# Two fp8 double-row matmuls, side by side or apart in a stream of bf16 matmuls

One core of one Trainium2 chip. The metric is device microseconds of one launch.

## The reference

Two stages, one after the other: cross-covariance attention over channels in 4 batches of 6016 tokens by 256 channels, then a gated feed-forward block on its 24064 output rows.

```python
def _attn_ref(q, k, v, tau):                       # 4 x 6016 x 256
    qn = q / (np.linalg.norm(q, axis=1, keepdims=True) + 1e-06)
    kn = k / (np.linalg.norm(k, axis=1, keepdims=True) + 1e-06)
    s = kn.transpose(0, 2, 1) @ qn / tau           # 256 x 256 a batch
    # ... softmax over the last axis -> a
    return v @ a

def _moe_ref(x, w_gate, w_val, w_out):             # 24064 x 256, 1536 wide
    g = x @ w_gate
    return (g * (1 / (1 + np.exp(-g))) * (x @ w_val)) @ w_out
```

## The kernel before

The attention matrix of a batch is multiplied into the gate and value weights (`Wg`, `Wv`), so the rows of v go straight into the feed-forward block. That block is a loop of steps: two gate matmuls and two value matmuls (512 columns each), then four output matmuls (256 columns) of the chunk before. Between the output matmuls of one step and the gate matmuls of the next stands the background work for the next batch, by a plan; among it is the product of q and k in fp8. In the double-row mode one matmul takes both 128-row slices of a pair at once.

```python
    def gemm1_pair(b, t):                       # one pair of 128-row slices
        # ... kq is allocated at t == 0
        for jh in range(CH):                    # CH = 2
            js = slice(jh * P, (jh + 1) * P)
            if pm == 2:
                nc.tensor.matmul(kq[:, jh, :], q_sb[:, ps:ps + 2, js],
                                 k_sb[:, ps:ps + 2, :], ..., perf_mode=DR)
            else:                               # the 47th slice has no partner
                nc.tensor.matmul(kq[:, jh, :], q_sb[:, ps, js], k_sb[:, ps, :], ...)

    def gv_matmuls(b, ci, f):
        # ... g_ps and v_ps from a pool of two buffers each
        for dst, W in ((g_ps, Wg), (v_ps, Wv)):
            for kk in range(CH):
                nc.tensor.matmul(dst[:, :mv], W[:, kk, fs], vT[:, kk, :mv], ...)
        return g_ps, v_ps, mv

    for t in range(NP):                         # NP = 24 pairs
        step = SQ0 + (5 * t) // 2
        plan[step].append((norm_acc, t))
        plan[step + 1].append((gemm1_pair, t))
    # ...
            g_ps, v_ps, mv = gv_matmuls(b, ci, f)
            # ... silu on ACT, product on DVE
            if prev is not None:
                prev.emit(prev.cm)              # four output matmuls
            if b + 1 < B:
                background(b + 1, ci * FH + f)  # the plan's work of this step
```

## Time and profile before

| | before |
|---|---|
| median of 6 runs (lowest to highest) | 815.43 us (815.32 to 816.31) |
| plain step, gate start to gate start | 1300 ns |
| step with a double-row pair, and the step after it | 1522.4 and 1310.9 ns |
| double-row pairs in batches 1 to 3 | 69, and 3 ordinary pairs |

The groups give the parts of TensorE's work that matter here; the columns are line, engine, operation, output and inputs, shapes and count, then busy us and mean ns of one, then idle us before them.

```profile
L463 PE MATMUL o_new<-w_out_sb,sv 128*128 128x256 bf16 x2256 | 338.3, 273 | 0.0
L429 PE MATMUL g_ps<-vT,Wg 128*128 128x512 bf16 (+1 forms) x1128 | 331.1, 375 | 0.0
L429 PE MATMUL v_ps<-vT,Wv 128*128 128x512 bf16 (+1 forms) x1128 | 330.4, 374 | 0.0
...
L149 PE MATMUL kq_new<-k_sb,q_sb 128*128 128x512 fp8e5 x184 | 40.0, 309 | 0.7 <-DMA q_sb<-in_q_dram 0.7
```

An output matmul is recorded with 273 ns, but the next one starts 109 ns after it: records overlap, since a matmul's end is modelled. What TensorE's stream costs is read from starts, not from these durations. The idle time of 0.0 says that nothing is waited for.

### The profile page before, as it was taken

What the parts mean: (1) busy time and instruction counts of PE and PEld (TensorE: products, weight loads), DVE (VectorE), ACT (ScalarE), POOL (GpSimd) and SP (SyncE); (2) the same over time, 40 slices, a digit from 0 to 9 for tenths busy, and PEclk for the clock granted to TensorE, in tenths of its full rate; (3) what the DMA queues carried; (4) which work ended last, traced back from release to release, by engine and by line L of the source; (5) the groups of instructions that cost most, each with busy time, mean ns of one, the idle gap of its engine ahead of it and who ended that gap; (6) DMA issues with size and microseconds to landing.
All of it is one profiled execution on the core that took longest, in us unless ns stands there. A gap on an engine that the chain in (4) does not pass through costs nothing.

```text
span 813.6 us, 13772 instructions
## 1 busy us (share of the span) xinstructions
PE 800.4 (98%) x5037; PEld 487.1 (60%) x5037; DVE 526.7 (65%) x816; ACT 434.9 (53%) x756; POOL 265.8 (33%) x344
## 2 busy tenths in 40 slices
PE   5999999999999999999999999999999999999998
PEld 3656666665565666666565666666656565665666
DVE  4777777667556777756756687765765555555554
ACT  4566655545555656545555556654554544444543
POOL 5515887313000888722000388751300000000000
PEclk9999999999999999999999999999999999999999
DMA  9993875328311678333812368632652112112101
GB/s 88 143 158 69 112 105 88 78 53 122 80 40 46 96 100 105 74 65 88 127 40 59 53 87 118 92 78 66 141 97 66 46 48 57 53 39 65 50 27 59
DMA packets 93220, 64.59 MB, mean 79 GB/s; under 512 B 52593, under 2 KB 92017, under 8 KB 92401
## 3 DMA queue, kind: packets, MB, share of 16 engines
q0 software_dynamic: 19200, 27.01, 28.6%
q1 hardware_dynamic: 73952, 36.71, 17.7%
q8 instruction: 39, 0.64, 0.3%
q14 instruction: 29, 0.23, 0.1%
HBM read 78.64 MB, written 36.70 MB: 142 GB/s over the span
## 4 chain that ended last, share of the span: by engine, by line
PE 95%; DMA 4%; POOL 1%; issue 0%; DVE 0%; POOLq 0%
PE o_new L463 30%; PE g_ps L429 30%; PE v_ps L429 30%; PE ps L398 2%; PE kq_new L149 2%; DMA v_sb<-in_v_dram 1%; DMA k_sb<-in_k_dram 1%; DMA q_sb<-in_q_dram 1%; POOL k_sb L104 1%; PE ps L331 0%; PE unit_ps L398 0%; PE cs L305 0%; PE kq_new L154 0%; PE ps L388 0%; PE vt_ps L128 0%
## 5 line engine op out<-in xcount | busy, mean ns | idle before, releaser
L439 DVE TENSOR_TENSOR sv<-silu,v_ps 128x512 bf16<-128x512 bf16 (+1 forms) x576 | 388.6, 675 | 263.2 <-ACT silu L435 261.4
L435 ACT ACTIVATE silu<-g_ps 128x512 bf16<-128x512 f32 (+1 forms) x576 | 338.6, 588 | 324.6 <-PE g_ps L429 302.0
L463 PE MATMUL o_new<-w_out_sb,sv 128*128 128x256 bf16 x2256 | 338.3, 273 | 0.0
L429 PE MATMUL g_ps<-vT,Wg 128*128 128x512 bf16 (+1 forms) x1128 | 331.1, 375 | 0.0
L429 PE MATMUL v_ps<-vT,Wv 128*128 128x512 bf16 (+1 forms) x1128 | 330.4, 374 | 0.0
L463 PEld LDWEIGHTS <-sv 128*128 128x128 bf16 x2256 | 220.7, 98 | 140.8
L429 PEld LDWEIGHTS <-Wv 128*128 128x128 bf16 x1152 | 112.7, 98 | 130.8 <-ACT Wv L410 0.2
L281 POOL TENSOR_TENSOR acc_new<-acc_new,sq 128x512 f32<-128x512 f32 x135 | 157.3, 1165 | 43.7 <-DVE sq L271 33.7
L429 PEld LDWEIGHTS <-Wg 128*128 128x128 bf16 x1152 | 106.7, 98 | 27.0 <-ACT Wg L410 0.2
L271 DVE TENSOR_TENSOR sq<-q_sb 128x512 bf16<-128x512 fp8e5 x72 | 63.9, 888 | 0.0
L276 POOL TENSOR_TENSOR acc_new<-sq 128x512 f32<-128x512 bf16 x3 | 3.5, 1152 | 150.7 <-DVE sq L271 150.7
L272 ACT ACTIVATE sq<-k_sb 128x512 bf16<-128x512 fp8e5 x72 | 44.2, 614 | 0.0
L149 PE MATMUL kq_new<-k_sb,q_sb 128*128 128x512 fp8e5 x184 | 40.0, 309 | 0.7 <-DMA q_sb<-in_q_dram 0.7
L472 ACT COPY o_sb<-o_new 128x512 f32<-128x512 f32 x48 | 28.1, 586 | 14.9 <-PE o_new L463 14.5
L474 DVE COPY o_sb<-o_new 128x512 f32<-128x512 f32 (+1 forms) x48 | 31.8, 661 | 3.0 <-PE o_new L463 3.0
L104 POOL DMA_DIRECT2D q_sb<-in_q_dram x48 | 27.0, 562 | 13.3 <-DMA k_sb<-in_k_dram 5.4
L104 POOL DMA_DIRECT2D k_sb<-in_k_dram x48 | 26.0, 549 | 11.3 <-DMA w_out_sb<-in_moe_w_out_dram 5.3
L176 PE MATMUL ss_new<-sq,ones_bf 128*128 128x256 bf16 x83 | 17.6, 351 | 9.0 <-ACT sq L166 8.4
L112 POOL DMA_DIRECT2D vb<-in_v_dram x47 | 24.1, 516 | 5.3 <-DMA vb<-in_v_dram 3.2
L149 PEld LDWEIGHTS <-q_sb 128*128 128x256 fp8e5 x184 | 22.1, 138 | 3.1 <-DMA q_sb<-in_q_dram 2.3
L176 PEld LDWEIGHTS <-ones_bf 128*128 128x128 bf16 x83 | 9.8, 121 | 15.7 <-issue 11.4
L351 POOL TENSOR_SCALAR den<-th 128x512 f32<-128x512 f32 x3 | 1.8, 612 | 51.8 <-ACT th L350 51.8
(93 smaller groups left out, 201.7 us busy)
## 6 DMA issues: line engine op xcount, KB each, us to landing
out_dram<-o_sb SPq DMA_DIRECT2D x92, 256.0 KB, 2.4
vb<-in_v_dram POOLq DMA_DIRECT2D x43, 256.0 KB, 5.4
k_sb<-in_k_dram POOLq DMA_DIRECT2D x44, 128.0 KB, 5.8
q_sb<-in_q_dram POOLq DMA_DIRECT2D x44, 128.0 KB, 5.0
w_out_sb<-in_moe_w_out_dram POOLq DMA_DIRECT2D x1, 768.0 KB, 13.5
vb<-in_v_dram POOLq DMA_DIRECT2D x4, 192.0 KB, 3.5
vT<-vb SPq DMA_TRANSPOSE x47, 3.8
w_gate_sb<-in_moe_w_gate_dram POOLq DMA_DIRECT2D x2, 256.0 KB, 7.3
```

The source lines that it names most:

```text
L104: nc.gpsimd.dma_start(out=dst[:, gs:gs + gm, :], in_=src[b].rearrange("(p s) c -> p s c", s=NS)[:, gs:gs + gm, :])
L149: nc.tensor.matmul(kq[:, jh, :], q_sb[:, ps:ps + 2, js], k_sb[:, ps:ps + 2, :], start=(t == 0 and jh == 0), stop=last, perf_mode=DR, skip_ ...
L176: nc.tensor.matmul(state[b, "ss", which], ones_bf, sq[:, s, :], start=(t == 0 and s == 0), stop=(t == t_last and s == pm - 1))
L271: nc.vector.tensor_mul(sq[:, :pm, 0, :], q_sb[:, ps:ps + pm, :], q_sb[:, ps:ps + pm, :])
L272: nc.scalar.activation(sq[:, :pm, 1, :], k_sb[:, ps:ps + pm, :], ACT.Square)
L281: nc.gpsimd.tensor_tensor(out=acc, in0=acc, in1=sq[:, s, :, :], op=ALU.add)
L429: nc.tensor.matmul(dst[:, :mv], W[:, kk, fs], vT[:, kk, :mv], start=(kk == 0), stop=(kk == CH - 1))
L435: nc.scalar.activation(silu[:, :mv], g_ps[:, :mv], ACT.Silu)
L439: nc.vector.tensor_mul(sv[:, f, :mv], silu[:, :mv], v_ps[:, :mv])
L463: nc.tensor.matmul(self.o_ps[:, j % 2, :], self.sv[:, f, j * P:(j + 1) * P], w_out_sb[:, f, :], start=(f == 0), stop=(f == FH - 1))
L472: nc.scalar.copy(o_sb[:, :m, :], self.o_ps[:, :m, :])
L474: nc.vector.tensor_copy(o_sb[:, :m, :], self.o_ps[:, :m, :])
```

## The change

The matmuls of a pair leave the plan. The first goes behind the two gate matmuls, the second behind the two value matmuls of the same step. The likely intent: a double-row matmul loads twice the weights, and this longer load is to lie under a 512-column matmul in place of the shorter double-row one.

```diff
-    def gemm1_pair(b, t):
+    def gemm1_pair(b, t, jhs=range(CH)):
...
-        if t == 0:
+        if t == 0 and 0 in jhs:
...
-        for jh in range(CH):
+        for jh in jhs:
...
-    def gv_matmuls(b, ci, f):
+    def gv_matmuls(b, ci, f, pair=None):
...
-        for dst, W in ((g_ps, Wg), (v_ps, Wv)):
+        for n, (dst, W) in enumerate(((g_ps, Wg), (v_ps, Wv))):
             for kk in range(CH):
                 nc.tensor.matmul(dst[:, :mv], W[:, kk, fs], vT[:, kk, :mv],
                                  start=(kk == 0), stop=(kk == CH - 1))
+            if pair is not None:
+                gemm1_pair(b + 1, pair, (n,))
...
-        plan[step + 1].append((gemm1_pair, t))
+        pair_at[step + 1] = t
...
-            g_ps, v_ps, mv = gv_matmuls(b, ci, f)
+            pair = pair_at.get(ci * FH + f) if b + 1 < B else None
+            g_ps, v_ps, mv = gv_matmuls(b, ci, f, pair)
```

More of the change, by code (lines that the diff above doesn't have):

```diff
@@ L479 @@
     plan = [[] for _ in range(STEPS)]
+    pair_at = {}
     for g in range(len(groups)):
```

## The prediction

> **What bounds the kernel now.** I read the engine table first, then the clock row of the slices, then the chain that ended last, and only then single instructions in the order of time.
>
> ```profile
> span 813.6 us, 13772 instructions
> PE 800.4 (98%) x5037; PEld 487.1 (60%) x5037; DVE 526.7 (65%) x816; ACT 434.9 (53%) x756; POOL 265.8 (33%) x344
> PEclk9999999999999999999999999999999999999999
> PE 95%; DMA 4%; POOL 1%; issue 0%; DVE 0%; POOLq 0%
> ```
>
> TensorE is 98% busy, holds 95% of the chain, and has its full clock in every slice; the 4% of DMA are the loads of the first 38 us. "Busy" alone proves little, because matmul ends are modelled, so I used the distance from one matmul's start to the next one's, from the trace's own starts in ns (the views print hundredths of a us). After the first 38 us: gate to value and value to value 216 ns, output to output 109 ns, with hardly any spread. A plain step (two gate, two value, four output matmuls) takes 1300 ns from gate start to gate start (mean of 297 steps, 1296 to 1300), and 4 x 216 + 4 x 109 = 1300. So nothing waits: the time is the sum of matmul spacings, and a change to the order of matmuls is worth only what it changes in the spacings.
>
> The pairs concerned: each of batches 1 to 3 has 24 pairs, 23 with the fp8 double-row mode (128x512 moving elements, 256 output columns) and a last one with ordinary fp8 matmuls (47 slices of rows is odd). That is 69 double-row pairs and 3 ordinary ones. This stretch has a double-row pair:
>
> ```profile
> 302.45 0.59 PE L429 MATMUL g_ps<-vT,Wg 128*128 128x512 bf16 x2
> 302.88 0.59 PE L429 MATMUL v_ps<-vT,Wv 128*128 128x512 bf16 x2
> 303.32 0.60 PE L463 MATMUL o_new<-w_out_sb,sv 128*128 128x256 bf16 x4
> 303.67 0.46 PE L149 MATMUL kq_new<-k_sb,q_sb 128*128 128x512 fp8e5 x2
> 303.98 0.61 PE L429 MATMUL g_ps<-vT,Wg 128*128 128x512 bf16 x2
> ...
> 305.29 0.38 PE L429 MATMUL g_ps<-vT,Wg 128*128 128x512 bf16 x1
> ```
>
> And this one an ordinary fp8 pair of the same 256 output columns, in the same place of the step:
>
> ```profile
> 534.94 0.59 PE L429 MATMUL g_ps<-vT,Wg 128*128 128x512 bf16 x2
> ...
> 536.24 0.38 PE L154 MATMUL kq_new<-k_sb,q_sb 128*128 128x256 fp8e5 x2
> 536.46 0.59 PE L429 MATMUL g_ps<-vT,Wg 128*128 128x512 bf16 x2
> ...
> 537.76 0.59 PE L429 MATMUL g_ps<-vT,Wg 128*128 128x512 bf16 x2
> ```
>
> From the gate before the pair to the gate one step after it: 2.84 us with the double-row pair, 2.82 us with the ordinary one. In ns, over all of them: the step that holds a double-row pair takes 1522.4 (69 of them), and the step after it 1310.4 in place of 1300. With the ordinary pair it is 1518 (= 1300 + 2 x 109) and then 1300. So a double-row pair costs 222.4 + 10.5 = 232.9 ns, of which 218 are its two matmuls, and **14.9 ns are lost**. The question is which of its neighbourhoods loses them. The weight loads tell:
>
> ```profile
> 303.65 0.25 PEld L149 LDWEIGHTS <-q_sb 128*128 128x256 fp8e5 x2
> 303.97 0.12 PEld L429 LDWEIGHTS <-Wg 128*128 128x128 bf16 x2
> ...
> 536.14 0.21 PEld L154 LDWEIGHTS <-q_sb 128*128 128x128 fp8e5 x2
> 536.35 0.21 PEld L429 LDWEIGHTS <-Wg 128*128 128x128 bf16 x2
> ```
>
> After ordinary fp8 the gate's first weight load starts at 536.35, 0.11 us ahead of its matmul at 536.46: it lies under the matmul before. After the double-row pair it starts at 303.97, just ahead of the matmul at 303.98: in ns, 109 after the second double-row matmul's start, that is when that matmul has streamed, and not 2 ns after its start as everywhere else. So the load of ordinary weights is not pulled under a double-row matmul. The two double-row loads, by contrast, begin 109 ns apart and are hidden, the second under the first double-row matmul. The first batch's product, where four double-row matmuls stand in a row, says the same: three spacings of 109, then 114 and 120 to the two ordinary matmuls behind (218 would be free; 16 lost once for four). The loss belongs to leaving the mode, not to a double-row matmul behind another.
>
> **What the Trainium skill says.** "TensorE: Matmul & The Clock Gate", section "Back-to-back issue gap", gives N / 2.4 + 2.5 ns: 216 for 512 columns and 109 for 256. The trace agrees to the ns. The same page, "Weight-path perf modes — Fast Weight Load (FWL) and DoubleRow", says that DoubleRow and fast weight load exclude each other and that DoubleRow pays 72% more for its weight load and 13% for its matmul. Here the double-row load lasts 137 ns against 98 (40% more), and the matmul's spacing is 109 ns, no more than bf16 of 256 columns. That longer load is the likely ground for the change: 137 ns do not fit under a 109 ns matmul, but under a 216 ns one. The recorded 137 contain latency, however: the chain of four keeps 109. The page's "Step-by-step: what each phase is for" has the pulling of a weight load ahead of the matmul in flight; the trace agrees between all ordinary neighbours and for double-row behind double-row, and not at the exit. No page states a cost for the exit.
>
> **The change part by part.**
> - Removed and added: no instruction. 144 fp8 matmuls move, 138 of them double-row.
> - Before: output, DR, DR, gate. One entry (output to DR), one DR behind DR, one exit. Entry and DR behind DR together: 28.3 + 190.0 = 218.3 ns of spacing, 0.1 more than 2 x 109 (the first start is recorded early; the sum is what counts). Exit: 14.9.
> - After: gate, gate, DR, value, value, DR, output. Two entries, each from a 216 ns matmul, which hides the 137 ns load with more room; they cost 0 now and can gain nothing. Two exits, one to a value matmul of 512 columns, one to an output matmul of 256. The exit measured to 512 columns costs 14.9, the one to 256 columns (first batch) 16; I take 15 for both.
> - So a pair loses 30 in place of 15: 69 x 14.9 ns = +1.03 us. The 3 ordinary pairs change nothing (109 each wherever they stand).
> - Beside TensorE: value matmuls of a pair's step end about 124 ns later than now relative to the gate. The product needs silu as well, which begins after the second gate matmul and takes 0.6 us, while both value matmuls end about 0.43 + 0.12 us after that; so the product's start stays with silu. Gate and value have two buffers each, and a value buffer's product (303.71, 0.69 long) is over at 304.40, over 1 us before its next use at about 305.7. No new wait.
> - The fp8 matmuls come up to 0.8 us earlier in their step. Their q and k land at least 7.8 us before their first use (smallest over all groups of batches 1 to 3), so no DMA wait.
>
> Sum: 815.44 + 1.03 = 816.47 us.
>
> **The rivals.**
> 1. The intent holds: a double-row load is exposed when it stands behind another double-row matmul, and splitting hides it. Then 14.9 ns a pair are saved: 814.4 us. For it: the 137 ns record. Against: the chain of four, where three such loads cost nothing, and the place of the late load (the gate's, not the second q's). No lone double-row matmul exists in the trace before, so this is not excluded; I give it 1 in 8.
> 2. The exit costs only at the first load after several double-row matmuls, or hides partly behind a lone one: 815.4 us, no change. 1 in 10.
> 3. A mode change inside a step costs more than at its end, for instance because the value matmul's wait for its buffer now stands at the exit, or since the load for double-row is not pulled under a 512-column matmul (109 ns exposed twice a pair would be +15 us, to 830). The entry now, at 0.1 ns, speaks against it. 3 in 100.
> 4. A wait of an engine for its buffer, from the shifted value matmuls: the slack above, some 1 us against a shift of 0.12, speaks against it.
>
> **Range and chances.** The largest credible mechanisms are worth 1 us either way out of 815, far inside 2% (16.3 us). The three runs of before lie between 815.43 and 816.31, so 0.9 us of scatter comes on top of a median. I take 816.5, and 815.3 to 817.6 for 8 in 10: this takes in rival 2 and leaves out rival 1. Within 2%: 98.5%; only rival 3 could go past it.
>
> **What would show it.** Right: in the trace after, a step with a double-row pair takes about 1548 ns (1300 + 218 + 30) and the step after it 1300; each ordinary weight load behind a double-row matmul starts about 109 ns after that matmul's start, and the two matmuls behind it lose 15 ns together. Busy time, clock and the other engines stay. Wrong: a pair's step at 1518 with no late load (rival 1), or at 1533 (rival 2), or starts of the value matmuls that wait for DVE (rivals 3 and 4).

## The result, and the profile after

816.71 us median of 6 runs (816.45 to 817.78) against 815.43: ratio 1.0017, 95% interval 1.0004 to 1.003. The ratio is the mean time of the one kernel's runs over that of the other's of the same rounds, so not quite the ratio of the medians. The interval is just clear of 1.

| | before | after |
|---|---|---|
| median | 815.43 us | 816.71 us |
| step with a double-row pair | 1522.4 ns (69) | 1548.2 ns (69) |
| step after it | 1310.9 ns | 1300.1 ns |
| the pair's cost over plain steps | 233.3 ns | 248.3 ns |
| of this over 2 x 109 | 15.3 ns | 30.3 ns |

These are means of distances between recorded starts, in ns, over all such steps. The difference, 15.0 ns a pair, times 69 is 1.03 us. (The prediction's 1310.4, and so its 232.9 and 14.9, average 72 steps: the three behind ordinary pairs, 1300 each, are among them.)

First the engine table and the double-row group of the changed kernel:

```profile
span 815.5 us, 13772 instructions
PE 802.4 (98%) x5037; PEld 483.6 (59%) x5037; DVE 525.2 (64%) x816; ACT 434.1 (53%) x756; POOL 265.9 (33%) x344
...
L149 PE MATMUL kq_new<-k_sb,q_sb 128*128 128x512 fp8e5 x184 | 71.6, 420 | 0.8 <-DMA q_sb<-in_q_dram 0.8
```

The same 184 double-row matmuls now show 71.6 us of busy time in place of 40.0, 420 ns each in place of 309. This is not 31.6 us of work: a lone double-row matmul is recorded as begun 28 ns after the 512-column matmul ahead of it, which still streams for 188 ns. A reader who went by the groups' busy time would be wrong by a factor of 30.

The order of time, TensorE alone, around one pair of the changed kernel (start us, length us, then the instructions):

```profile
303.85 0.59 PE L429 MATMUL g_ps<-vT,Wg 128*128 128x512 bf16 x2
304.09 0.46 PE L149 MATMUL kq_new<-k_sb,q_sb 128*128 128x512 fp8e5 x1
304.39 0.60 PE L429 MATMUL v_ps<-vT,Wv 128*128 128x512 bf16 x2
304.65 0.46 PE L149 MATMUL kq_new<-k_sb,q_sb 128*128 128x512 fp8e5 x1
304.95 0.61 PE L467 MATMUL o_new<-w_out_sb,sv 128*128 128x256 bf16 x4
305.40 0.60 PE L429 MATMUL g_ps<-vT,Wg 128*128 128x512 bf16 x2
305.83 0.59 PE L429 MATMUL v_ps<-vT,Wv 128*128 128x512 bf16 x2
```

From gate to gate 1.55 us, and from gate to value afterwards 0.43 as in any plain step: both losses are now inside the step. The weight loads of the same stretch say where:

```profile
304.07 0.14 PEld L149 LDWEIGHTS <-q_sb 128*128 128x256 fp8e5 x1
304.39 0.12 PEld L429 LDWEIGHTS <-Wv 128*128 128x128 bf16 x2 [0.19 <-issue]
304.62 0.14 PEld L149 LDWEIGHTS <-q_sb 128*128 128x256 fp8e5 x1
304.95 0.33 PEld L467 LDWEIGHTS <-sv 128*128 128x128 bf16 x4 [0.19 <-issue]
305.29 0.21 PEld L429 LDWEIGHTS <-Wg 128*128 128x128 bf16 x2
```

The double-row load (304.07) lies under the gate matmul ahead of it, as intended. But the value weights load at 304.39, together with the matmul that needs them, and so do the output weights at 304.95. An ordinary load is 0.11 us or more ahead of its matmul elsewhere (305.29 for the gate at 305.40). Before, there was one such late load a pair, that of the gate; now there are two. Averaged over the pairs, the late loads start 325.1 ns (value) and 325.0 ns (output) after the start of the 512-column matmul ahead of the double-row one, and 216 + 109 is 325: they wait until the double-row matmul has streamed, and no longer. The entry into double-row thus adds nothing, and the exit everything.

The waits of the changed kernel list it (who waited for what: us in total, times, longest us); the kernel before has neither line:

```profile
PEld L429 <- issue: 12.9, 69, 0.2
PEld L467 <- issue: 12.9, 69, 0.2
```

These 2 x 12.9 us are idle time of the weight loader, 0.19 us each time, nearly all of it beside matmuls. What reaches the stream is 14.9 ns at each of the 69 exits to a value matmul and 15.1 at each of the 69 to an output matmul; in the kernel before, measured in the same way, it is 15.0 at each of the 69 exits to a gate matmul, which stand at the end of a step. (The table's 15.3 and 30.3 hold about 0.3 ns more, from taking 216 and 109 as whole ns.) Each 15 has two parts: the matmul starts 4 ns after its late load, and the matmul behind it comes 11 ns late.

The 4 and the 11 are not special to double-row. Twice at the start of the kernel before, an ordinary load is late because its data is: the gate's at 38.36 us (waiting for ACT) and one at 40.73 (waiting for a DMA). Its 512-column matmul starts 4 ns after it, and the next one 226 and 227 ns after that in place of 216. That suggests that 15 ns is what any load costs here that is not pulled ahead; what marks the exit is that at none of the 207 (69 before, 138 after) it is.

**The ordinary pairs as a control.** Each kernel has three pairs of ordinary fp8 matmuls that the change moves in the same way. The changed kernel's:

```profile
536.85 0.59 PE L429 MATMUL g_ps<-vT,Wg 128*128 128x512 bf16 x2
537.28 0.27 PE L154 MATMUL kq_new<-k_sb,q_sb 128*128 128x256 fp8e5 x1
537.39 0.60 PE L429 MATMUL v_ps<-vT,Wv 128*128 128x512 bf16 x2
537.82 0.27 PE L154 MATMUL kq_new<-k_sb,q_sb 128*128 128x256 fp8e5 x1
537.93 0.60 PE L467 MATMUL o_new<-w_out_sb,sv 128*128 128x256 bf16 x4
538.37 0.59 PE L429 MATMUL g_ps<-vT,Wg 128*128 128x512 bf16 x2
```

537.28 to 537.39 and 537.82 to 537.93 are the plain 0.11 us, and the whole step takes 1519.7 ns (mean of three) against 1518 before, where a double-row pair's goes from 1533 to 1548. Same place, same fp8 type ahead of bf16 weights, same shift of the value matmuls, without the mode: at most 2 ns in place of 15. So neither the place nor the type is what costs. One more place speaks against the type: at the end of the first batch's product, at 34.5 us, a double-row matmul is followed by an ordinary *fp8* one, and the next two starts come after 114 and 120 ns (before; 113 and 120 after) in place of 109 each: the same loss with the same type on both sides.

**The scatter of the runs.** The two profiled spans differ by 1.9 us, not by 1.03. The first gate matmul starts at 38.36 us before and at 39.33 after, and the change does not touch anything ahead of it. The stretch before it, first in the kernel before, then in the changed one:

```profile
35.94 0.81 PE L388 MATMUL ps<-warm_bf,ones_bf 128*128 128x512 bf16 x3
```

```profile
36.33 1.49 PE L388 MATMUL ps<-warm_bf,ones_bf 128*128 128x512 bf16 x3
```

The same three matmuls follow one another at 216 ns before and at 427 after: half the clock. The stretches of the two kernels, before first (us; busy us and count of PE, PEld, DVE, ACT, POOL; granted clock; share and GB/s of DMA):

```profile
34.00:36.00 2.00, 1.68 (x27) 1.26 (x28) 1.10 (x5) 1.02 (x4) 1.27 (x3) 1.00 1.40 190
36.00:38.00 2.00, 2.00 (x19) 1.09 (x17) 1.60 (x7) 1.07 (x3) 2.00 (x3) 1.00 1.28 220
```

```profile
34.00:36.00 2.00, 1.74 (x24) 1.27 (x24) 1.12 (x4) 1.05 (x4) 1.28 (x3) 0.68 1.40 190
36.00:38.00 2.00, 2.00 (x12) 1.11 (x11) 1.24 (x4) 0.91 (x2) 2.00 (x3) 0.50 1.27 217
```

In the changed kernel's profiled run the clock was halved from 34.72 to 38.13 us, for 3.413 us, a stretch that began while TensorE worked off the first batch's last slices as they came in; in the profiled run of before it was not. The profile's clock row shows 9 in every slice for both kernels: a slice of 20 us hides such a stretch. That this comes and goes by chance rather than with the change is an inference: both kernels issue the same instructions there, and other runs of the changed kernel have the full clock (1.000) and times of 816.45 to 816.64. The 0.97 us at the start and the 1.03 us of the exits, less 0.1 us from two of the first steps (one 0.21 shorter, one 0.11 longer), make the 1.9 us. The three changed runs of 816.45 to 816.64 have spans of 814.7 to 814.8 us at full clock against 813.6 of the profiled run of before, also at full clock: 1.1 to 1.2 us apart. Runs of before show a step of this size too (816.31 beside five at 815.32 to 815.46), though of these only the profiled run's clock is on record; and the slowest run of the changed kernel, 817.78, had the full clock, so there is another source of such a microsecond that I cannot name.

### The profile page after: what moved, and what is told of

Its sections match the earlier page's. It is cut to its first block, busy times and chain, and to the rows that moved or that the text cites. A ratio compares the mean times of both kernels' runs of the same rounds, so it can differ in the third digit from the quotient of the medians.

```text
span 815.5 us, 13772 instructions
## 1 busy us (share of the span) xinstructions
PE 802.4 (98%) x5037; PEld 483.6 (59%) x5037; DVE 525.2 (64%) x816; ACT 434.1 (53%) x756; POOL 265.9 (33%) x344
## 4 chain that ended last, share of the span: by engine, by line
PE 95%; DMA 4%; POOL 1%; issue 0%; DVE 0%; POOLq 0%
PE o_new L467 30%; PE v_ps L429 30%; PE g_ps L429 30%; PE ps L398 2%; PE kq_new L149 2%; DMA v_sb<-in_v_dram 1%; DMA k_sb<-in_k_dram 1%; DMA q_sb<-in_q_dram 1%; POOL k_sb L104 1%; PE ps L388 0%; PE unit_ps L398 0%; PE vt_ps L128 0%; PE ps L331 0%; PE cs L305 0%; PE kq_new L154 0%
## 5 line engine op out<-in xcount | busy, mean ns | idle before, releaser
L467 PEld LDWEIGHTS <-sv 128*128 128x128 bf16 x2256 | 214.8, 98 | 137.3 <-issue 12.9
L429 PEld LDWEIGHTS <-Wv 128*128 128x128 bf16 x1152 | 107.0, 98 | 127.3 <-issue 12.9
L429 PEld LDWEIGHTS <-Wg 128*128 128x128 bf16 x1152 | 111.9, 98 | 23.4 <-ACT Wg L410 0.2
L149 PE MATMUL kq_new<-k_sb,q_sb 128*128 128x512 fp8e5 x184 | 71.6, 420 | 0.8 <-DMA q_sb<-in_q_dram 0.8
L149 PEld LDWEIGHTS <-q_sb 128*128 128x256 fp8e5 x184 | 24.1, 138 | 18.6 <-DMA q_sb<-in_q_dram 2.4
```

Of the source, the lines that this page charges most:

```text
L149: nc.tensor.matmul(kq[:, jh, :], q_sb[:, ps:ps + 2, js], k_sb[:, ps:ps + 2, :], start=(t == 0 and jh == 0), stop=last, perf_mode=DR, skip_ ...
L467: nc.tensor.matmul(self.o_ps[:, j % 2, :], self.sv[:, f, j * P:(j + 1) * P], w_out_sb[:, f, :], start=(f == 0), stop=(f == FH - 1))
```

## The experiments

No experiment gave a result, so what is said here rests on the two traces.

Four kernels keep the double-row mode and only regroup its matmuls. They would have told place from number of exits, and would have tried a faster version.

Both matmuls side by side, between gate and value:

```diff
-            if pair is not None:
-                gemm1_pair(b + 1, pair, (n,))
+            if pair is not None and n == 0:
+                gemm1_pair(b + 1, pair)
```

> Both fp8 double-row matmuls of a pair stand side by side between the gate and the value matmuls: the middle of the step, but one exit from the double-row mode per pair. Exit theory (each exit to an ordinary matmul costs 15 ns, whatever the place): a pair's step takes 1300 + 218 + 15 = 1533 ns, the step after it 1300, and the time is that of before, 815.4 us. Place rival (fp8 in the middle of a step costs, at the end not): a step of about 1548 ns and 816.5 us, as in the changed kernel.

One matmul at the end of each of two steps:

```diff
-        plan[step + 1].append((gemm1_pair, t))
+        plan[step + 1].append((gemm1_pair, t, (0,)))
+        plan[step + 2].append((gemm1_pair, t, (1,)))
```

> The two matmuls of a pair apart, but each at the end of a step, behind the output matmuls, in two steps one after the other: two exits per pair, none in the middle of a step. Exit theory: 69 exits more than before, + 1.04 us: 816.5 us; each exit loses 15 ns at the two gate matmuls behind it. Place rival: no cost, 815.4 us, as before.

Gathered, two pairs at a time, and in a further kernel all 24 (`t % 24 == 23`):

```diff
-        plan[step + 1].append((gemm1_pair, t))
+        if t % 2 == 1:
+            for u in range(t - 1, t + 1):
+                plan[step + 1].append((gemm1_pair, u))
```

> Two pairs at the end of one step in every five, four double-row matmuls in a row, in place of one pair in every two or three steps: 36 exits in place of 69. Exit theory: 33 x 15 ns = 0.5 us less than before, 814.9 us. Rival of the change's intent (a double-row load behind a double-row matmul is what costs, about 15 ns each time): 36 bundles with three such places each, or two in the bundle that has the ordinary pair, 105 in place of 69: + 0.5 us, 815.9 us. The trace tells them apart: spacings inside the row of four at 109, or at 124.

> All 24 pairs of a batch at the end of one step, 46 double-row matmuls in a row (5.0 us): 3 exits in the whole stretch in place of 69. Exit theory: 66 x 15 ns = 1.0 us less than before, 814.4 us, as long as no other engine's wait appears behind the burst. Intent rival: 45 places a batch where a double-row load stands behind a double-row matmul in place of 23, + 1.0 us, 816.4 us. A third way: after 5 us without gate matmuls ACT and DVE have no work and the queue of the next loads moves, and a wait eats the gain: 815.4 or more.

Not run, all four. Nothing follows from them.

Four kernels without the mode, as controls of place, type and burst. Each double-row matmul becomes two ordinary ones:

```diff
-                nc.tensor.matmul(kq[:, jh, :], q_sb[:, ps:ps + 2, js],
-                                 k_sb[:, ps:ps + 2, :],
-                                 start=(t == 0 and jh == 0), stop=last,
-                                 perf_mode=DR, skip_group_check=True)
+                for s in range(2):
+                    nc.tensor.matmul(kq[:, jh, :], q_sb[:, ps + s, js],
+                                     k_sb[:, ps + s, :],
+                                     start=(t == 0 and jh == 0 and s == 0),
+                                     stop=last, skip_group_check=True)
```

on top of the kernel before (side by side), of the changed kernel (split), of the version with all between gate and value (mid), and with 12 pairs in a row.

> Every double-row matmul, the first batch's too, replaced by two ordinary fp8 matmuls of 256 columns; four per pair, side by side at the end of the step as before. Exit theory: ordinary matmuls have no exit, so a pair's step takes 1300 + 4 x 109 = 1736 ns and the next one 1300, no load is late, and batches 1 to 3 get 69 x (436 - 232.9) = 14.0 us longer; the first batch, which waits for its loads, adds 0 to 2: 829.4 to 831.4 us. Rival (the type costs: leaving fp8 weights for bf16 weights loses 15 ns): step after the pair at 1310, and 1 us more.

> The same four ordinary fp8 matmuls per pair, two behind the gate and two behind the value matmuls, as in the changed kernel. Exit theory: the place costs nothing without the mode: steps of 1736 and 1300 ns, the time that of the side-by-side version within 0.3 us, though the value matmuls are shifted by 218 ns, more than the 124 of the change. Place rival (the middle of a step, the shifted value matmuls or the buffers' waits cost 15 ns per pair): 1751 and + 1.0 us against side by side.

> The same four ordinary fp8 matmuls per pair, all between gate and value. Exit theory: again 1736 and 1300 ns, no difference from the other two. Buffer-wait rival: the value matmuls now come 436 ns later, 3.5 times the shift of the change; if the shift cost 15 ns there, over 15 would be lost here, + 1 us or more.

> The same ordinary matmuls, those of 12 pairs in a row at the end of one step (48 x 109 = 5.2 us), twice a batch. Exit theory: with no mode to leave, gathering gains nothing: the time of side by side within 0.3 us, if the burst raises no wait of another engine. If 5 us without gate matmuls cost a wait behind each of the 6 bursts, steps behind a burst are longer than 1300 ns; then gathering double-row pairs in this way would not pay either.

None of them ran on a chip: the four were sent in four times, and the split version alone four times more (its expectation then put the two other rivals in one sum: a step of 1766 ns), over several hours; each time it came back that no chip had run it, through no fault of the kernel. Nothing follows from them either. The question of the first three (does the place cost without the mode?) is answered on a small scale by the three ordinary pairs that each of the two traces holds; the fourth (does a burst of 5 us raise a wait?) stays open.

## Why the prediction was right

The predicted time was 816.5 us; measured, 816.71, inside the range of 815.3 to 817.6. Point by point:

- **The bound.** The prediction took the time as the sum of matmul spacings. The changed trace keeps them: plain steps 1300.0 ns (369 of them), and the extra time of the pairs' steps is all of the difference after the first few steps.
- **The cost of one exit.** Taken as 14.9 ns from the kernel before and carried over to exits of another kind, behind a lone double-row matmul. Measured 14.9 ns (value, 512 columns) and 15.1 (output, 256 columns), against 15.0 for the exits of the kernel before. This was the step with a risk in it, since the kernel before has no lone double-row matmul, and the evidence for rows of another length was thin: of the first batch's rows of four only one is followed at once by an ordinary matmul at full clock.
- **The number of exits.** One a pair became two, 69 to 138: + 1.03 us, as predicted. A pair's step was predicted at about 1548 and the next at 1300; they are 1548.2 and 1300.1.
- **The entries.** Predicted free, from a 512-column matmul as from a 256-column one. The late loads at 325.0 to 325.1 ns (216 + 109) show it.
- **Rival 1**, the intent (a saving of 14.9 ns a pair), falls: a step of 1518 without a late load would have been needed. The load of the second double-row matmul was never exposed. **Rival 2** (1533) falls too, and so does **rival 3** in its large form: the step would have been over 1.7 us.
- **Rival 4**, a wait for a buffer, did not appear: the idle time ahead of gate, value and output matmuls is 0.0 in the changed profile as before.
- **The size in the times.** Medians differ by 1.28 us, of which the exits give 1.03. The rest is within the scatter of runs, a part of which is the half clock at the start. That the median came within 0.3 us of the forecast is therefore partly luck; the agreement that counts is that of the steps.
- **Slips that changed nothing.** Besides the 1310.4 (above), entry and double-row behind double-row are 0.3 ns over 2 x 109, not 0.1. The fp8 matmuls start up to 0.98 us earlier in their step by the records, not 0.8, and the smallest time from landing to first use fell from 7.8 to 6.8 us: still no wait. And "full clock in every slice" overlooks the start: the clock's record begins at 21.33 us, and the double-row matmuls at 20 us are 213 ns apart, not 109.

What stays open: *why* an ordinary weight load is not pulled under a double-row matmul. The page "TensorE: Matmul & The Clock Gate" of the Trainium skill (section "Weight-path perf modes — Fast Weight Load (FWL) and DoubleRow") says that DoubleRow and fast weight load exclude each other. It says so of how one instruction's weights are loaded, not of the hand-over, so that this is why the load waits is a guess; no run here tests it. Also open: whether gathering the pairs gains what the exit theory says. An estimate from the 14.9 ns: four in a row (36 exits) would save 33 x 14.9 ns = 0.5 us, all 46 of a batch in a row (3 exits) 66 x 14.9 ns = 1.0 us. No such version ran, so neither is claimed to be faster.

## What to carry to other kernels

In a stream of matmuls that never waits, count the places where double-row matmuls hand over to ordinary ones: here each cost 15 ns, whether one or two double-row matmuls stood ahead of it and wherever in the step it was, so a pair is better kept together than split (longer rows were not run in this stream). Before moving a matmul to hide a long weight load, look whether that load is exposed at all: a record of 137 ns was longer than the 109 ns matmul above it and still cost nothing. And for differences of a microsecond, measure the distance between starts in the trace; medians with a scatter of one microsecond barely resolve them, and busy times of pipelined matmuls mislead.

## What the Trainium skill lacked or had wrong

- "TensorE: Matmul & The Clock Gate", section "Weight-path perf modes — Fast Weight Load (FWL) and DoubleRow", gives no cost for going back to ordinary matmuls. Here: 14.9 to 15.1 ns at each of 138 exits, with the ordinary load held until the double-row matmul has streamed. Its figures for the mode itself, measured at N = 512, were too high for this kernel's 256 columns: the load is recorded with 137 ns against 98 (40% more, not 72%), and the matmul's spacing is 109 ns as for bf16 of 256 columns (not 13% more).
- The same page, "Back-to-back issue gap", sets a sustained spacing of about 131 ns for pairs of load and matmul at N = 512, and calls the 216 ns of its formula N / 2.4 + 2.5, which it gives for an isolated matmul, an over-count. This kernel's stream, fully pipelined and each matmul with a load of its own, keeps 216 ns: the prediction used the formula, and it was right to the ns.
- The same page, "Why this matters for your kernels", asks for no idle gap of over about 3 us and has the clock fall back after an idle window. In one run here it was halved for 3.413 us (the page's window length) without such a gap: in the 3.4 us ahead and just before, matmuls started at most 1.03 us apart (from 31.01 to 32.03, waiting for q from a DMA), but by their columns they streamed for only about 1.3 of these 3.4 us (an estimate: columns over 2.4 GHz, the page's clock). It cost about 1 us of one run. The row alone misses this; the page's section "A second HAM failure mode: psum-queue depth-cycling" does tell of short idles that bring the clock down, without saying how much idle it takes.
